# Retention with a routed expert layer: one pool of four PSUM banks for outputs, transposes and states, the router's tasks in other places of a batch, and an order of its own for the first batch

## The chip, the cores and the metric

The kernel runs on one core of a Trainium2 chip. The metric is the time of one execution on the device in microseconds (us), the median over several runs. Below, PE is TensorE (matmuls; PEld its weight loads), DVE is VectorE, ACT is ScalarE, POOL is GpSimd, and SP issues most of the DMA transfers, in its own order.

## The reference

All arrays are float32. A retention layer (attention without softmax, with a decay per head) feeds a layer of eight experts, of which each token uses one.

```python
# q, k, v: (8 batches, 8 heads, 576 positions, 64)
scores = (1 / np.sqrt(64)) * np.matmul(q, k.transpose(0, 1, 3, 2))
gamma = 1.0 - 2.0 ** (-5.0 - np.arange(8))
rel = pos[:, None] - pos[None, :]
Dmat = np.where(rel >= 0, gamma[:, None, None] ** rel, 0.0)
attn = np.matmul(scores * Dmat, v)
x = attn.transpose(0, 2, 1, 3).reshape(4608, 512)        # tokens

xn = x / (norm(x) + 1e-6);  en = expert_emb / (norm(expert_emb) + 1e-6)
logits = xn @ en.T / tau                                 # (4608, 8)
expert_idx = argmax(logits);  gate_w = softmax(logits)[expert_idx]
for e in range(8):                                       # w1: 512 x 1024, w2: 1024 x 512
    out[mask] = gate_w[mask, None] * (np.maximum(x[mask] @ w1[e], 0) @ w2[e])
```

## The kernel before

The work has two stages. In the **batch stage** the eight batches are worked through one after the other. A batch has four head pairs p (two heads side by side on 128 partitions) and four chunks c of 128 positions with a tail of 64. For each pair, `emit_A` (L582) multiplies k and q of each chunk, and DVE multiplies the result with the decay (L591) into a tile `raw`. `emit_O` (L640) multiplies that with v into an output bank. `emit_U` (L609) forms each chunk's state from k and v; ACT copies the first (L619) and DVE sums the others (L621) into `Tst`, so that `Tst[c]` holds all chunks up to c. `emit_S` (L657) adds state times query to the output banks, and ACT copies these to the token tiles `xT` and `xC` (L665 to L668). The tail goes through `emit_At` (L677), a product on DVE that gives `pt` (L679), and `emit_Ot` (L692, L695). POOL scales the queries (`scale_q`, L571) and the keys (`scale_k`, L552) with powers of gamma; for the queries it first builds the table `gsb` (L514). In batch 0 the keys aren't loaded: PE transposes them out of the q/k tiles (`turn_k`, L560), and DVE scales them (L562). `build_E` makes the scaled expert embeddings `E32` (L527 to L537; the reciprocal norm goes through a power on POOL, L533). `keep_warm` issues small matmuls that only keep PE busy.

Between these stand the **router's tasks** for the batch before: `route_logits` (L736), `route_tile` (four transposes L716, a copy to `y` L720, a store of 128 tokens L722, a sum of squares on ACT L724), `route_turn` (L749, reduced on DVE L752), `route_head` (on DVE, L175 to L183, the largest logit), `route_rank` (PE L234 to L238, then DVE L241 to L261), `route_onehot` (L269 to L284) and `route_table` (L297, added on DVE L308). With the last table, rows of x are gathered for the first expert (`gather`, L336).

In the **expert stage** each expert has five tiles of 128 rows; mm1 (L393) and mm2 (L884) multiply in three passes of split float32 weights. ACT and DVE split the weights as they arrive (`wsplit_tasks`, L149 and L150); those of the first expert's w1 are split within the batch stage.

The order on PE is the order in which the program is written (`manual_schedule` for PE). On the other engines the scheduler orders by the program and by when it thinks that inputs are there; each engine then works in a fixed order, and so does SP. A tile of a pool takes the slot that the scheduler gave it and waits for the reader of the tile that was there. PSUM has eight banks: four for `psa` (names a), two for `pso` (outputs, o), two for `psm` (everything else, m).

## Time and profile before

| | |
|---|---|
| median of 3 runs | 656.71 us (655.44 to 658.6) |
| profiled execution | 653.69 us, span of its instructions 651.9 us |
| PE busy | 614.0 us, 94% of the span |
| DVE, ACT, POOL busy | 322.9, 240.4, 211.2 us |
| first decay matmul (L582) of batches 1, 2, 3, 4, 5, 6, 7 | 43.26, 63.26, 87.35, 107.02, 128.56, 147.92, 168.32 us |
| mean granted clock of PE | 0.984 |

The profiled execution's own time lies under the median of the runs by 3.0 us. Times in the trace count from the start of the span. A batch is taken to begin with its first decay matmul.

### The profile page before, as it was taken

Reading aid. Unit: us, or ns where it says so; the run is one execution under the profiler, and the core shown is the slowest. Engines: PE = TensorE matmul, PEld = TensorE weight load, DVE = VectorE, ACT = ScalarE, POOL = GpSimd, SP = SyncE. Lnnn points to the kernel's source line nnn. Section 1 sums busy time; section 2 is a strip of 40 time slices with the busy share of each in tenths; the row PEclk is TensorE's granted clock in tenths of the full one; section 3 lists DMA queues with packets and bytes.
Section 4 is the critical chain, followed back from the end, with each engine's and each line's share of the span. In section 5 each row is a group of like instructions: output and inputs, shape, how many; then the busy total and the mean of one; then the engine's idle time right before and its main releaser. Section 6 shows DMA issues by size and latency. Waiting matters only on the chain. (4 is left out here: it accounts for less than half of the span.)

```text
span 651.9 us, 12713 instructions
## 1 busy us (share of the span) xinstructions
PE 614.0 (94%) x5273; PEld 549.4 (84%) x5273; DVE 322.9 (50%) x612; ACT 240.4 (37%) x457; POOL 211.2 (32%) x190
## 2 busy tenths in 40 slices
PE   4779789999879999999999999999999999999996
PEld 4768677888759898988998998899899889989985
DVE  2455667556546777581465167157336706822200
ACT  0124363444534455442443234143233514422211
POOL 0853335422134663503323240350324135010011
PEclk9879999999989999999999999999999999999999
DMA  8848997757225789565159148526704833610001
GB/s 310 330 166 315 310 336 264 266 206 276 83 81 179 217 208 306 151 164 210 46 115 285 58 120 173 193 71 135 270 31 114 260 111 98 139 57 25 1 33 44
DMA packets 73997, 110.08 MB, mean 169 GB/s; under 512 B 44714, under 2 KB 45774, under 8 KB 72144
## 3 DMA queue, kind: packets, MB, share of 16 engines
q1 hardware_dynamic: 66256, 89.28, 43.9%
q0 software_dynamic: 7680, 19.95, 9.2%
q8 instruction: 42, 0.69, 0.5%
q14 instruction: 19, 0.16, 0.1%
HBM read 80.62 MB, written 19.94 MB: 154 GB/s over the span
## 5 line engine op out<-in xcount | busy, mean ns | idle before, releaser
L393 PE MATMUL a<-xs,wslot 128*128 128x384 f32 (+1 forms) x1536 | 228.2, 310 | 0.2 <-ACT xs L358 0.2
L393 PEld LDWEIGHTS a<-xs,wslot 128*128 128x128 f32 x1536 | 225.8, 189 | 1.2 <-ACT xs L358 0.5
L884 PE MATMUL o<-wslot,hs 128*128 128x512 f32 (+1 forms) x984 | 222.0, 386 | 0.0
L884 PEld LDWEIGHTS o<-wslot,hs 128*128 128x128 f32 x984 | 181.1, 188 | 38.3
L858 DVE SCALAR_TENSOR_TENSOR hs<-a,hs 128x384 fp32r<-128x384 f32 (+1 forms) x128 | 62.6, 490 | 166.9 <-ACT hs L857 166.2
L892 POOL DMA_INDIRECT out<-y,sid x40 | 43.7, 1092 | 223.9 <-ACT y L891 195.0
L857 ACT ACTIVATE hs<-a 128x384 fp32r<-128x384 f32 (+1 forms) x128 | 55.9, 438 | 125.0 <-PE a L393 124.4
L150 DVE TENSOR_TENSOR wslot<-raw,wslot 128x1024 fp32r<-128x1024 f32 x64 | 78.2, 1222 | 31.0 <-ACT wslot L149 31.0
L149 ACT CAST wslot<-raw 128x1024 fp32r<-128x1024 f32 x64 | 66.8, 1043 | 51.4 <-DMA raw<-w 51.4
L891 ACT ACTIVATE y<-o,gt 128x512 f32<-128x512 f32 (+1 forms) x41 | 27.6, 676 | 109.4 <-PE o L884 82.3
L336 POOL DMA_INDIRECT raw<-xd,gid x40 | 41.7, 1043 | 72.8 <-DVE wslot L150 38.4
L571 POOL TENSOR_TENSOR qkt<-qkt,gsb 128x448 f32<-128x448 f32 x32 | 36.5, 1159 | 68.4 <-PE a L582 68.3
L591 DVE TENSOR_TENSOR raw<-a,cs 128x512 f32<-128x512 f32 x64 | 39.9, 681 | 28.8 <-PE a L582 28.8
L347 POOL DMA_INDIRECT gt<-gd,gid x40 | 49.7, 1244 | 12.2 <-issue 11.9
L640 PE MATMUL o<-raw,vt 128*64 128x128 f32 x512 | 35.2, 284 | 8.5 <-DVE raw L591 8.2
L640 PEld LDWEIGHTS o<-raw,vt 128*64 128x64 f32 x512 | 30.0, 142 | 11.4 <-issue 9.3
L552 POOL TENSOR_TENSOR kt<-kt,cs 128x512 f32<-128x512 f32 x28 | 28.3, 1039 | 29.4 <-DMA kt<-kv 29.4
L582 PE MATMUL a<-qkt 64*128 64x128 f32 x512 | 33.2, 279 | 2.2 <-DMA qkt<-qk 2.2
L582 PEld LDWEIGHTS a<-qkt 64*128 64x128 f32 x512 | 29.9, 188 | 4.7 <-DMA qkt<-qk 2.4
L381 DVE COPY raw<-raw 128x1024 uint16<-128x1024 uint16 x37 | 28.1, 781 | 3.6 <-DMA raw<-raw 3.6
L720 ACT COPY y<-m 128x512 f32<-128x512 f32 x34 | 19.4, 585 | 22.3 <-PE m L716 14.4
L374 DVE COPY raw<-raw 128x1024 uint16<-128x1024 uint16 x37 | 26.1, 718 | 3.1 <-DMA raw<-xd,gid 3.1
(128 smaller groups left out, 418.6 us busy)
## 6 DMA issues: line engine op xcount, KB each, us to landing
raw<-w SPq DMA_DIRECT2D x64, 512.0 KB, 5.1
qkt<-qk SPq DMA_DIRECT2D x32, 576.0 KB, 6.4
xd<-y SPq DMA_DIRECT2D x36, 256.0 KB, 4.3
vt<-kv SPq DMA_DIRECT2D x7, 1152.0 KB, 7.1
kt<-kv SPq DMA_DIRECT2D x7, 1024.0 KB, 6.0
vt<-kv SPq DMA_DIRECT2D x4, 256.0 KB, 6.1
cs<-cst SPq DMA_DIRECT2D x5, 128.0 KB, 5.2
raw<-xd,gid POOLq DMA_INDIRECT x40, 3.6
```

What stands on the lines that cost most here:

```text
L149: nc.scalar.copy(hi, raw)
L150: nc.vector.tensor_tensor(out=sl[:, 1, c * 1024 : (c + 1) * 1024], in0=raw, in1=hi.bitcast(F32), op=ALU.subtract)
L336: return nc.gpsimd.indirect_dma_start(out=t[:, :DM], out_offset=None, in_=xd[:rows, :], in_offset=bass.IndirectOffsetOnAxis(ap=gid[:, a : ...
L347: nc.gpsimd.indirect_dma_start(out=g[:, i : i + 1], out_offset=None, in_=gd[:, :], in_offset=bass.IndirectOffsetOnAxis(ap=gid[:, a : a + 1 ...
L393: nc.tensor.matmul(ps[:, :n], w[:, ws, d, f * P : (f + 1) * P], x[:, xsp, d, :], start=(d == 0 and k == 0), stop=(d == NP - 1 and k == 2),)
L582: nc.tensor.matmul(ps[h][:, c * P : (c + 1) * P], t[hs, 1, c * P : (c + 1) * P], t[hs, 0, c * P : (c + 1) * P], start=True, stop=True,)
L591: nc.vector.tensor_tensor(out=pm[:, h], in0=ps[h].rearrange("p (c n) -> p c n", c=NCH), in1=decay[:, 2 * p + h].unsqueeze(1).broadcast_to( ...
L640: nc.tensor.matmul(po[h * D : (h + 1) * D, c * P : (c + 1) * P], v[:, c, 2 * p + h, :], pm[:, h, c, :], start=(c == 0), stop=False,)
L857: a = nc.scalar.activation(hi, ps[:, :n], AF.Relu)
L858: v = nc.vector.scalar_tensor_tensor(out=hs[:, 1, f, o : o + n], in0=ps[:, :n], scalar=0.0, in1=hi.bitcast(F32), op0=ALU.max, op1=ALU.subt ...
L884: nc.tensor.matmul(ps[:, :step], hs[:, hsp, f, i * P : (i + 1) * P], w[:, ws, f, n : n + step], start=(f == 0 and k == 0), stop=(f == NF - ...
L892: nc.gpsimd.indirect_dma_start(out=out[:, :], out_offset=bass.IndirectOffsetOnAxis(ap=sid[:, a : a + 1], axis=0), in_=y, in_offset=None, b ...
```

## The change

The two pools `pso` and `psm` become one pool of four banks. The second state tile `Tst` goes, and `y` has five buffers instead of three. The constants that only the batch stage uses get a tile of their own, `cd`, in the batch stage's memory.

`emit_U(b)` moves from batch b-1 into batch b, ahead of `emit_O(b, 0)`. The keys are loaded at other times through this: their buffer is free when an earlier U has read it. The router's tasks stand in named slots of a batch: logits and two tiles, then ranks, ahead of U; turn, a tile, the head and the table of the batch before that ahead of the outputs of pairs 2 and 3; the other tiles at the end. The squares L724 of a slot stand behind all its copies. For batch 6 the tasks come earlier: logits and two tiles already at its own end. The splits of the first weights move from batches 1 to 4 into batches 4 and 5.

Batch 0 has an order of its own: `build_E` first, then two `turn_k`, the outputs of pairs 0 and 1, then pairs 2 and 3. The expert embeddings and tau are loaded third and fourth from the start, the constants of `gsb` ahead of the fourth q/k tile.

PE at the start of batch 0, behind the first decay matmuls and the warm ones. Names: qkt a q/k tile, kt keys, vt values, raw decay products, sq squares of the embeddings. Before:

```order
L560 MATMUL m<-ident,qkt 128x128 x16
L609 MATMUL m<-vt,kt 64x64 x32
L640 MATMUL o<-raw,vt 64x128 x16
L657 MATMUL o<-qkt,Tst_197 64x128 x12
L530 MATMUL m<-sq,onef 128x8 x4
L582 MATMUL a<-qkt 128x128 x16
```

After:

```order
L530 MATMUL m<-sq,onef 128x8 x4
L560 MATMUL m<-ident,qkt 128x128 x8
L640 MATMUL m<-raw,vt 64x128 x16
L582 MATMUL a<-qkt 128x128 x16
L560 MATMUL m<-ident,qkt 128x128 x8
L609 MATMUL m<-vt,kt 64x64 x32
L657 MATMUL m<-qkt,Tst 64x128 x12
```

The embeddings' matmul, one half of the transposes and the first outputs now stand ahead of the states.

DVE at the same place, before:

```order
L591 TENSOR_TENSOR raw<-a,cs 128x512 x4
L527 TENSOR_TENSOR sq<-emb 128x32
L562 TENSOR_TENSOR kt<-m,cs 128x4x128 x4
L621 TENSOR_TENSOR Tst_197<-m,Tst_197 128x256 x3
L532 COPY en<-m 128x8
L534 TENSOR_SCALAR en<-en,taub 128x8
L535 RECIPROCAL en<-en 128x8
L537 TENSOR_TENSOR E_204<-emb,en 128x8 x4
L591 TENSOR_TENSOR raw<-a,cs 128x512 x4
```

After:

```order
L527 TENSOR_TENSOR sq<-emb 128x32
L591 TENSOR_TENSOR raw<-a,cd 128x512 x4
L532 COPY en<-m 128x8
L534 TENSOR_SCALAR en<-en,taub 128x8
L535 RECIPROCAL en<-en 128x8
L537 TENSOR_TENSOR E_201<-emb,en 128x8 x4
L591 TENSOR_TENSOR raw<-a,cd 128x512 x4
L562 TENSOR_TENSOR kt<-m,cs 128x4x128 x4
L621 TENSOR_TENSOR Tst<-m,Tst 128x256 x3
```

The embedding's chain (sq, en, E) now stands ahead of the second half of the decay products, and the keys kt behind them.

DVE in batch 3 from the sums of the states to the next batch (tab the slot table; L_all, mx, w, wm, oh, s belong to the head). Before:

```order
L621 TENSOR_TENSOR Tst_197<-m,Tst_197 128x256 x3
L679 TENSOR_TENSOR pt<-m,cs 128x256
L308 TENSOR_TENSOR tab<-m,tab 128x80
L752 TENSOR_REDUCE L_all<-m 128x32
L175 TENSOR_REDUCE mx<-L_all 128x4
L176 TENSOR_TENSOR L_all<-L_all,mx 128x32
L178 SCALAR_TENSOR_TENSOR w<-L_all,wme 128x32
L180 TENSOR_REDUCE wm<-w 128x4
L182 TENSOR_TENSOR oh<-wm,wme 128x32
L183 TENSOR_SCALAR tok_all<-wm 128x4
L241 TENSOR_REDUCE s_1466<-oh 128x8
```

After:

```order
L621 TENSOR_TENSOR Tst<-m,Tst 128x256 x3
L591 TENSOR_TENSOR raw<-a,cd 128x512 x4
L759 TENSOR_REDUCE L_all<-m 128x32
L308 TENSOR_TENSOR tab<-m,tab 128x80
L175 TENSOR_REDUCE mx<-L_all 128x4
L176 TENSOR_TENSOR L_all<-L_all,mx 128x32
L178 SCALAR_TENSOR_TENSOR w<-L_all,wme 128x32
L180 TENSOR_REDUCE wm<-w 128x4
L182 TENSOR_TENSOR oh<-wm,wme 128x32
L183 TENSOR_SCALAR tok_all<-wm 128x4
L241 TENSOR_REDUCE s_1425<-oh 128x8
L679 TENSOR_TENSOR pt<-m,cd 128x256
```

The tail product pt stood ahead of the turn's reduction, the table and the head; now it stands behind them.

The diff, cut to its core (line numbers in the text are those of the kernel before; behind the change the tile's copy is still L720, its squares are L730, the turn L756 and L759, the logits L743):

```diff
-    my = ctx.enter_context(tc.tile_pool(name="my", bufs=3))
+    my = ctx.enter_context(tc.tile_pool(name="my", bufs=5))
     psa = ctx.enter_context(tc.tile_pool(name="psa", bufs=4, space=PSUM))
-    pso = ctx.enter_context(tc.tile_pool(name="pso", bufs=2, space=PSUM))
-    psm = ctx.enter_context(tc.tile_pool(name="psm", bufs=2, space=PSUM))
+    psm = ctx.enter_context(tc.tile_pool(name="psm", bufs=4, space=PSUM))
...
         load_qk(0, 0)
         load_decay(0)
-        nc.sync.dma_start(out=cs[:, :_FIRST], in_=cst[:, :_FIRST])
+        nc.sync.dma_start(out=cs, in_=cst[:, :_FIRST])
+        nc.sync.dma_start(out=emb, in_=embT)
+        nc.sync.dma_start(out=taub, in_=tau.rearrange("(o n) -> o n", o=1).broadcast_to([P, 1]))
         load_qk(0, 1)
         load_decay(1)
         load_v(0, True)
         load_qk(0, 2)
         load_decay(2)
+        o = _C["g1"][0]
+        nc.sync.dma_start(out=cd[:, o - _FIRST :], in_=cst[:, o:])
         load_qk(0, 3)
         load_decay(3)
-        o = _C["g1"][0]
-        nc.sync.dma_start(out=cs[:, o:], in_=cst[:, o:])
         load_decay(4)
         kt[0] = a1.tile([P, KW], F32, name="kt", bufs=2)
-        nc.sync.dma_start(out=emb, in_=embT)
-        nc.sync.dma_start(out=taub, in_=tau.rearrange("(o n) -> o n", o=1).broadcast_to([P, 1]))
...
-        Tst = [ap.tile([P, NCH, NP, D], F32, name=f"Tst{i}") for i in range(2)]
+        Tst = ap.tile([P, NCH, NP, D], F32, name="Tst")
...
-                po = Po[b, p] = pso.tile([P, 512], F32, name="o")
+                po = Po[b, p] = psm.tile([P, 512], F32, name="m")
...
-            junk = a2.tile([P, DM], BF16, name="junk", bufs=1)
-            nc.scalar.activation(junk, xw, AF.Square, accum_out=ss_all[:, t : t + 1])
+            squares.append((xw, t))
...
-            first, second = owed or ([], [])
-            owed[:] = [rank], [table]
-            if b == B - 2:
...
-            return [[logits] + first + tiles[:2], second + [turn, head] + tiles[2:]]
+            if b == B - 2:
+                gathers = [lambda i=i: gather(0, i, group_tiles(B - 1)[0] * P) for i in range(3)]
+                return {
+                    (b, 3): [logits] + tiles[:2] + [sq],
+                    (b + 1, 0): [turn] + tiles[2:3] + [head, sq],
+                    (b + 1, 1): [rank, onehot] + tiles[3:] + [sq],
+                    (b + 1, 2): [],
+                    (b + 1, 4): [table, lambda: slots_to_tokens(0, 3)] + gathers + [route_bump],
+                }
+            return {
+                (b + 1, 0): [logits] + tiles[:2] + [sq],
+                (b + 1, 2): [turn] + tiles[2:3] + [head, sq],
+                (b + 1, 3): tiles[3:] + [sq],
+                (b + 2, 0): [rank, onehot],
+                (b + 2, 2): [table],
+            }
...
         for b in range(B):
-            for g in range(2):
-                if b + 1 < B:
-                    load_qk(b + 1, 2 * g)
-                    if g == 0:
-                        load_v(b + 1)
-                        load_k(b + 1)
-                        scale_k(b + 1)
-                    load_qk(b + 1, 2 * g + 1)
-                for p in (2 * g, 2 * g + 1):
+            if b + 1 < B:
+                load_qk(b + 1, 0)
+                load_qk(b + 1, 1)
+                load_v(b + 1)
+                load_k(b + 1)
+            for p in (0, 1):
+                emit_A(b, p)
+                scale_q(b, p)
+            if b == 0:
+                keep_warm(NW2)
+                build_E()
+                turn_k(0)
+                turn_k(1)
+                emit_O(0, 0)
+                for p in (2, 3):
+                    emit_A(0, p)
+                    scale_q(0, p)
+                turn_k(2)
+                turn_k(3)
+                emit_U(0)
+            else:
+                slot(b, 0)
+                emit_U(b)
+                emit_O(b, 0)
+            emit_S(b, 0)
+            if b + 1 < B:
+                load_qk(b + 1, 2)
+                load_qk(b + 1, 3)
+                scale_k(b + 1)
+            slot(b, 1)
+            if b > 0:
+                for p in (2, 3):
                     emit_A(b, p)
                     scale_q(b, p)
-
-                if b == 0 and g == 0:
-                    keep_warm(NW2)
-                    for p in range(NP):
-                        turn_k(p)
-                    emit_U(0)
-                if g == 0:
-                    slot()
-                elif b + 1 < B:
-                    emit_U(b + 1)
-                else:
-                    slot()
-                emit_O(b, g)
-                if g == 1:
-                    emit_At(b)
-                emit_S(b, g)
-                if b == 0 and g == 0:
-                    build_E()
-                if g == 0:
-                    if b == B - 1:
-                        slot()
-                else:
-                    emit_Ot(b)
-                    if b < B - 1:
-                        slot()
-                if b > 0 and wq:
-                    wq.pop(0)()
-            if b < B - 1:
-                tasks += route_tasks(b)
+            slot(b, 2)
+            emit_O(b, 1)
+            slot(b, 4)
+            emit_At(b)
+            emit_S(b, 1)
+            emit_Ot(b)
+            slot(b, 3)
+            if b > 3 and wq:
+                wq.pop(0)()
+                wq.pop(0)()
+        assert not slots
...
-                ps = pso.tile([P, 512], F32, name="o")
+                ps = psm.tile([P, 512], F32, name="m")
```

More of the change, by code (lines that the diff above doesn't have):

```diff
@@ L722, in route_tile, with route_squares @@
             nc.sync.dma_start(out=xd[t * P : (t + 1) * P, :], in_=xw)
-            junk = a2.tile([P, DM], BF16, name="junk", bufs=1)
-            nc.scalar.activation(junk, xw, AF.Square, accum_out=ss_all[:, t : t + 1])
+            squares.append((xw, t))
+        squares = []
+        def route_squares():
+            for xw, t in squares:
+                junk = a2.tile([P, DM], BF16, name="junk", bufs=1)
+                nc.scalar.activation(junk, xw, AF.Square, accum_out=ss_all[:, t : t + 1])
+            squares.clear()
         ltb = {}
@@ L771, in route_tasks @@
             if b == B - 2:
-                return [
-                    [logits] + first + tiles[:2] + [turn, head] + second,
-                    tiles[2:3] + [rank],
-                    tiles[3:] + [table, lambda: slots_to_tokens(0, 3)]
-                    + [lambda i=i: gather(0, i, group_tiles(B - 1)[0] * P) for i in range(3)]
-                    + [route_bump],
-                ]
-            return [[logits] + first + tiles[:2], second + [turn, head] + tiles[2:]]
-        tasks = []
+                gathers = [lambda i=i: gather(0, i, group_tiles(B - 1)[0] * P) for i in range(3)]
@@ L782, in retention_moe, with slot @@
+        slots = {}
+        for b in reversed(range(B - 1)):
+            for k, v in route_slots(b).items():
+                slots.setdefault(k, []).extend(v)
         wq = wsplit_tasks(0)
-        def slot():
-            if tasks:
-                for task in tasks.pop(0):
-                    task()
+        def slot(b, k):
+            for task in slots.pop((b, k), ()):
+                task()
         ordered = tc.manual_schedule(engines={mybir.EngineType.PE})
```

29 lines of the change are left out of this document (16 added, 13 removed).

## The prediction

> **What bounds the kernel now.** I read the span by stage first: busy time of each engine in four stretches, cut where the first decay matmul of batch 1 and of batch 7 starts (43.26 and 168.32) and where the expert matmuls run without a break (203.15). After the stretch and its length stand PE, PEld, DVE, ACT and POOL busy, the granted clock, the DMA share and GB/s.
>
> ```profile
> 0.00:43.26 43.26, 28.46 (x432) 26.10 (x432) 17.32 (x38) 4.37 (x7) 21.84 (x25) 0.84 0.69 258
> 43.26:168.32 125.06, 113.54 (x1987) 97.25 (x1983) 75.12 (x177) 58.02 (x137) 42.95 (x40) 1.00 0.77 273
> 168.32:203.15 34.83, 29.89 (x358) 23.55 (x358) 18.32 (x59) 18.01 (x46) 8.23 (x7) 0.95 0.30 106
> 203.15:651.90 448.75, 442.11 (x2508) 402.47 (x2505) 212.19 (x338) 159.96 (x269) 138.22 (x118) 1.00 0.48 136
> ```
>
> The last stretch is 69% of the span, with PE busy in 442 of 448.75 us at full clock. The change gives its outputs four banks instead of two; there is nothing there to win, and I cost it at nothing. All that can move lies in the first 203 us: PE idles 14.8 us in the first stretch, whose clock is 0.84, 11.5 us in the six batches 1 to 6, 4.9 us in the rest. The list of waits, for PE between 43 and 189 us, names the largest:
>
> ```profile
> PE m L716 <- DVE t L248: 5.6, 5, 1.9
> ```
>
> Token-tile transposes (L716) wait for a bank that holds the ranks until L248 has read them, behind four decay products on DVE. In the first batch the timeline in order of time shows two holes of PE (start, length, work, idle time before it and its releaser):
>
> ```profile
> 15.46 3.61 POOL L514 TENSOR_TENSOR gsb<-cs 128x448 f32<-128x448 f32 x4 [15.04 <-DMA emb<-embT]
> 16.05 0.39 DVE L527 TENSOR_TENSOR sq<-emb 128x32 f32<-128x32 f32 x1 [5.54 <-DMA emb<-embT]
> 16.36 1.28 DVE L562 TENSOR_TENSOR kt<-m,cs 128x512 f32<-128x512 f32 x2
> 17.09 1.97 PE L560 MATMUL m<-ident,qkt 128*128 128x128 f32 x8 [6.22 <-DVE kt L562]
> 18.99 2.93 PE L609 MATMUL m<-vt,kt 128*64 128x64 f32 x64
> 28.10 1.67 POOL L533 TENSOR_TENSOR en<-en,half 128x8 f32<-128x8 f32 x1
> 31.17 3.81 DVE L537 TENSOR_TENSOR E<-emb,en 128x8 f32<-128x8 f32 x4
> 35.73 4.18 PE L640 MATMUL o<-raw,vt 128*64 128x128 f32 x32 [5.61 <-DVE raw L591]
> 43.26 2.06 PE L582 MATMUL a<-qkt 64*128 64x128 f32 x32
> ```
>
> The first hole ends at 17.09: turn_k needs a bank that L562 frees, and L562 stands on DVE behind the squares of the expert embeddings, the seventeenth load on SP. The second ends at 35.73: the output matmuls wait for decay products queued on DVE behind the gate vector's power on POOL (28.10) and four tiny products (31.17) that took 3.81 us while POOL was scaling.
>
> **The change, part by part.** *First batch.* Durations for a walk through its new order:
>
> ```profile
> 8.02 1.16 PE L582 MATMUL a<-qkt 64*128 64x128 f32 x16 [2.22 <-DMA qkt<-qk]
> 9.22 1.29 DVE L591 TENSOR_TENSOR raw<-a,cs 128x512 f32<-128x512 f32 x2 [2.01 <-PE a L582]
> 9.83 1.04 PE L560 MATMUL m<-ident,qkt 128*128 128x128 f32 x8
> 21.75 1.92 PE L640 MATMUL o<-raw,vt 128*64 128x128 f32 x32
> 23.60 1.53 PE L657 MATMUL o<-qkt,Tst 64*64 64x128 f32 x24
> 25.05 1.06 PE L530 MATMUL m<-sq,onef 128*128 128x8 f32 x8
> 28.03 2.08 PE L609 MATMUL m<-vt,kt 128*64 128x64 f32 x64
> ```
>
> The embeddings and tau now precede the second q/k tile on SP, so I put A(0,1) 0.3 late, at 8.3. Twelve warm matmuls follow as before, then build_E (1.06, new here), then two turn_k (1.04): instead of 9.83 the turns start at 11.2, and O(0,0) at 12.2; its 1.92 end at 14.1, A(0,2) and A(0,3) (2.06) at 16.2. The power starts on POOL near 11.4 and ends at 13.1 (1.67); the growth factors gsb, whose constants now load before the fourth q/k tile, follow until 16.7 (3.61). So the tiny products again meet a busy POOL: 1.4 us after the power (as from 29.77 to 31.17) plus 3.81 gives 18.3. Only then come the decay products of pairs 2 and 3 (2 x 1.29: 20.9) and the four key products (2 x 1.28: 23.4). With all four banks held, the last two turn_k wait for the first two key products, so PE is idle from 16.2 to about 21.5, and U(0) ends near 25.5 (2.08 warm, 2.93 cold). The sums let S(0,0) end at 27.4, O(0,1) at 29.3. From the end of O(0,1) to batch 1 took 43.26 - 39.91 = 3.35 before. Batch 1 then starts at 33: **10.3 us earlier**, of which 2.08 is U(1), now done in batch 1. If the tiny products are not held, 30; if cold PE and late loads add up, 37. The fourth q/k tile now loads behind the constants of gsb; PE wants it only at 15. The keys of batch 2 load only after U(0), and hold POOL for the queries of batch 1: 25.5 + 7.3 to land (below) + 4.04 + 2.24 is 39, and S(1,0) wants them at 41.
>
> *Batches 1 to 6* took 125.06 us. How short a batch is without its waits, for an odd and an even one:
>
> ```profile
> 128.56 2.06 PE L582 MATMUL a<-qkt 64*128 64x128 f32 x32
> 132.77 1.09 PE L716 MATMUL m<-ident,xT 128*128 128x128 f32 x8 [0.91 <-DVE t L248]
> 147.92 2.06 PE L582 MATMUL a<-qkt 64*128 64x128 f32 x32
> 151.67 0.18 PE L234 MATMUL m<-oh,stri 128*128 128x32 bf16 x1 [0.48 <-ACT lt L739]
> 165.37 0.77 PE L749 MATMUL m<-ident,lt 128*128 128x128 f32 x5 [0.22 <-ACT xC L700]
> 166.41 1.09 PE L716 MATMUL m<-ident,xT 128*128 128x128 f32 x8 [0.28 <-DVE L_all L752]
> 168.32 2.06 PE L582 MATMUL a<-qkt 64*128 64x128 f32 x32
> ```
>
> Batch 5 took 19.36 with a wait of 0.91, so 18.4; batch 6 took 20.40 with 0.48, 0.22 and 0.28, so 19.4. Three of each make 113.4: **11.6 us** of waits and slower stretches go if nothing replaces them. I think they do go: U(b) now stands between the ranks and O(b,0), so nobody waits for the bank of the ranks, and the weight splits, which put DVE behind a load in batches 1 and 2, move to batches 4 and 5. Each batch still has one U, so that is even. The new wait is on DVE: the head of the router (L175 to L241) stood behind the tail product pt and now stands in front of it, and PE needs pt for the tail outputs L692.
>
> ```profile
> 156.22 2.06 PE L582 MATMUL a<-qkt 64*128 64x128 f32 x32
> 157.41 2.48 DVE L591 TENSOR_TENSOR raw<-a,cs 128x512 f32<-128x512 f32 x4 [3.24 <-PE a L582]
> 162.70 0.42 DVE L679 TENSOR_TENSOR pt<-m,cs 128x256 f32<-128x256 f32 x1 [1.48 <-PE m L677]
> 163.80 0.28 PE L692 MATMUL m<-pt,vt 64*64 64x64 f32 x4
> ```
>
> From the decay matmuls of pairs 2 and 3 (156.22) to L692 were 7.58 us with a U of 2.08 in them; without it, and with turn and one tile added (L716, eight transposes in 1.09, so about 1.1 for both), PE arrives 6.6 us after 156.22. DVE starts its products 1.19 us after PE and needs 2.48 for them: 3.67. Then the head:
>
> ```profile
> 85.09 0.39 DVE L752 TENSOR_REDUCE L_all<-m 128x32 f32<-128x128 f32 x2 [0.64 <-PE m L749]
> 89.03 0.21 DVE L241 TENSOR_REDUCE s<-oh 128x8 f32<-128x40 bf16 x1
> 166.06 0.39 DVE L752 TENSOR_REDUCE L_all<-m 128x32 f32<-128x128 f32 x2 [0.64 <-PE m L749]
> 167.65 0.23 DVE L241 TENSOR_REDUCE s<-oh 128x8 f32<-128x40 bf16 x1
> ```
>
> First and last row of the head: 4.15 us with POOL scaling keys (L552, below), 1.82 without. So pt (0.42) is there at 8.2 or at 5.9: a wait of 1.6 per batch, or none. Which? POOL scales the keys of two batches ahead in these very microseconds:
>
> ```profile
> 77.77 0.33 SPq L446 DMA_DIRECT2D kt<-kv  x1
> 85.04 4.04 POOL L552 TENSOR_TENSOR kt<-kt,cs 128x512 f32<-128x512 f32 x4 [7.85 <-DMA kt<-kv]
> 89.05 2.24 POOL L571 TENSOR_TENSOR qkt<-qkt,gsb 128x448 f32<-128x448 f32 x2
> ```
>
> The keys' load was issued at 77.77, as U had just freed the buffer, and POOL began 7.3 us later. U(b) now ends some 6.5 us into the batch (2.06, an estimated 2.4 for logits, two tiles and ranks, 2.08), so POOL starts near 14; O and S (1.92 + 1.53) bring the next decay matmuls to 10, and the head starts at 10 + 3.67. They meet in batches 1 to 5. The first reductions may still be ahead of POOL, so I take 1.1 instead of 1.6: **+5.5** (0 to 8.2).
>
> The Trainium skill, "SBUF — State Buffer", "Who interferes with whom", says that a DVE instruction with two SBUF inputs, or in a 2-port mode, is blocked for the whole of a GpSimd instruction that reads SBUF, and that reductions and instructions with one SBUF input are not. By that rule L176, L178, L182 and L183 could each lose a whole scaling, and the term would be +16.8 where the rows give at most +8.2, the sum -2 instead of -13.3. The 4.15 above decide against it: each operation there lost only the rest of a scaling.
>
> *Splits.* Four casts stand on ACT ahead of copies out of PSUM in batches 4 and 5:
>
> ```profile
> L149 ACT CAST wslot<-raw 128x1024 fp32r<-128x1024 f32 x64 | 66.8, 1043 | 51.4 <-DMA raw<-w 51.4
> ```
>
> At 1.04 each that is 0 to 4.2; ACT was busy 58 of 125 us, so I take **+1**. *Batch 7 and after:* U(7) comes in (**+2.1**, L609); logits and two tiles go to batch 6, even; its waits for the gathered rows stay, since the slot table still ends behind the last decay products. *Costed at nothing:* squares behind copies (two squares now stand on ACT ahead of U's first copy, which S(b,0) wants only after O(b,0)), five y buffers, the cd tile, one Tst (U(b) writes it after batch b-1 has read it), q/k loads at other places of SP (eight buffers, a batch ahead). If that cover goes, their price is that of the second rival.
>
> Sum: -10.3 - 11.6 + 5.5 + 1 + 2.1 = -13.3. The profiled execution took 653.69 (span 651.9), so 640.4; the median of the runs is 3.0 above it, so **643.4**.
>
> **The rivals.** (a) *No collision:* keys land later than the head. For it: 166.06 shows the head in 1.82. Against: the load follows U at once. 643.4 - 5.5 = 638. (b) *The batches win nothing:* four banks in turn tie every step to the reader four tiles back, and ACT's squares and copies become the waits. For it: the total number of banks is the same. Against: before, two banks served all small tiles. Then 11.6 - 5.5 - 1 is lost: 648.5. (c) *Full holds:* four operations of the head each lose a whole scaling, 4.04 / 4 = 1.01: the head takes 1.82 + 4.04 = 5.86, pt comes at 3.67 + 5.86 + 0.42 = 9.95, PE waits 3.35 in each of five batches, 16.8 instead of 5.5: 654.7. Against: 4.15 with POOL scaling throughout. (The skill's rule above would allow it.) (d) *The first batch does not do what it says:* DVE's chain (tiny products, then decay, then keys) also moves U behind 25.5, and only 4 us are won: 649.5. (e) *Slower:* keys late. POOL is in order, so keys of b+2 that land late hold the queries of b+1 (2.24), which S(b+1,0) needs about 8.4 us into its batch. By the rows keys land 7.3 us after U, and POOL is through with keys and queries (4.04 + 2.24) some 2 us into the next batch at most, so this decides only when landing takes 6 to 7 us longer, 14 instead of 7.3; each further us costs five. To undo 13.3 and add 0.5% takes 3.3 us more: landing after 17 us gives 660.
>
> **How the numbers follow.** Forecast 0.42; (a) 0.20; (b) 0.18; (c) 0.07; (d) 0.07; (e) 0.06. No change within 0.5% (3.3 us, about what the measurement can tell) means 653.4 to 660. The forecast, (a), (b) and (d) are below: 0.87. (c) is no change, 0.07; (e) is slower, 0.06. The range takes in (a) with the first batch at 30 instead of 33 (635), less what splits may save, and (b) and (d) with a little on top: 633 to 652.
>
> **What would show it.** Right: the first L582 of batch 1 near 33; PE holes before 21.5 and before L692 in batches 1 to 5, released by pt, about 1 us each; no wait of L716 for L248; batch 7 starting near 155; the expert stage unchanged at 449. Wrong: batch 1 after 37; L609 or L640 waiting for copies on ACT in every batch; L657 waiting for POOL's queries.

## The result, and the profile after

The changed kernel took 632.86 us in the median of four runs (631.27 to 634.45), beside 656.08 for the kernel before on the same chip: a ratio of 0.9641 with a 95% interval of 0.9602 to 0.9681. The forecast was 643.4 with a range of 633 to 652; the median lies at its lower end, 0.1 us outside. The sign was right; the gain is 23 us instead of 13. The profiled execution took 632.18, its span is 630.4, so 21.5 less than the 651.9 before.

First the stretches, cut where the same work starts: the first decay matmul of batch 1, that of batch 7, and the first mm2. The last two stretches of before (the first two stand in the prediction), with the columns as there:

```profile
168.32:216.40 48.08, 42.98 (x437) 36.18 (x437) 28.89 (x92) 24.01 (x57) 16.36 (x10) 0.96 0.37 128
216.40:651.90 435.50, 429.01 (x2425) 389.83 (x2424) 201.62 (x306) 153.97 (x257) 130.09 (x115) 1.00 0.47 135
```

And the four of after:

```profile
0.00:31.75 31.75, 26.48 (x367) 24.13 (x367) 12.47 (x35) 4.00 (x6) 14.21 (x18) 0.89 0.87 319
31.75:149.63 117.88, 113.42 (x2004) 99.75 (x2000) 68.98 (x177) 58.82 (x141) 53.78 (x48) 0.99 0.83 301
149.63:194.48 44.85, 42.03 (x484) 38.44 (x484) 28.66 (x95) 22.15 (x54) 15.72 (x10) 0.96 0.39 131
194.48:630.40 435.92, 429.21 (x2425) 389.82 (x2424) 201.75 (x306) 153.69 (x257) 132.75 (x115) 1.00 0.47 135
```

The first batch gave 11.5 us, batches 1 to 6 gave 7.2, batch 7 with the passage to the experts 3.2, and the expert stage took 0.4 more. PE is busy for nearly the same time in batches 1 to 6 (113.54 and 113.42), but the span there shrank to 117.88: the idle time is what went. The list of waits after, for PE between 31 and 182 us:

```profile
PE m L716 <- ACT xT L665: 2.2, 1, 2.2
PE m L640 <- DVE L_all L759: 1.8, 3, 0.6
PE m L640 <- DVE raw L591: 1.5, 1, 1.5
```

No wait of L716 for L248 is left, and none of L692 for pt, which the prediction had put in its place. The largest one left is behind a weight split on ACT. The first batch in order of time:

```profile
13.40 1.67 POOL L533 TENSOR_TENSOR en<-en,half 128x8 f32<-128x8 f32 x1 [12.98 <-DVE en L532]
15.60 1.15 DVE L537 TENSOR_TENSOR E<-emb,en 128x8 f32<-128x8 f32 x4
15.67 3.67 POOL L514 TENSOR_TENSOR gsb<-cd 128x448 f32<-128x448 f32 x4 [0.61 <-DMA cd<-cst]
19.51 1.28 DVE L562 TENSOR_TENSOR kt<-m,cs 128x512 f32<-128x512 f32 x2
20.34 1.22 PE L560 MATMUL m<-ident,qkt 128*128 128x128 f32 x8 [2.06 <-DVE kt L562]
31.75 2.06 PE L582 MATMUL a<-qkt 64*128 64x128 f32 x32
```

PE's hole is where it was expected, ahead of the last two turns (L560), but 2.06 long instead of 5.3. The tiny products L537 took 1.15 instead of 3.81. They began at 15.60, and POOL began the growth factors (L514) at 15.67, held until then by the load of their constants: one of the four products took 0.91 us beside the first factor, the other three some 0.16 each.

The head and the tail product in batch 1, with the keys' load ahead of them and POOL's scaling behind:

```profile
38.98 0.48 SPq L445 DMA_DIRECT2D kt<-kv  x1
40.98 2.06 PE L582 MATMUL a<-qkt 64*128 64x128 f32 x32
44.57 0.28 DVE L759 TENSOR_REDUCE L_all<-m 128x32 f32<-128x128 f32 x1
46.01 0.21 DVE L241 TENSOR_REDUCE s<-oh 128x8 f32<-128x32 bf16 x1
46.61 0.42 DVE L679 TENSOR_TENSOR pt<-m,cd 128x256 f32<-128x256 f32 x1 [0.19 <-PE m L677]
47.71 0.28 PE L692 MATMUL m<-pt,vt 64*64 64x64 f32 x4
49.15 4.05 POOL L552 TENSOR_TENSOR kt<-kt,cs 128x512 f32<-128x512 f32 x4 [4.66 <-DMA kt<-kv]
```

The head (L759 to L241) ran in 1.65 us, and pt ended at 47.03, 0.68 before L692. POOL took the keys up at 49.15: issued 7.2 us into the batch and 10.2 on their way. The prediction had 6.5 and 7.3, which put POOL beside the head. In batches 1 to 5 POOL began 8.5 to 10.2 us after the issue, and 1.1 to 2.9 us after the end of the head.

### The profile page after: what moved, and what is told of

It reads as the page before. It is cut to its first block, busy times and chain, and to the rows that moved or that the text cites. A ratio compares the mean times of both kernels' runs of the same rounds, so it can differ in the third digit from the quotient of the medians.

```text
span 630.4 us, 12840 instructions
## 1 busy us (share of the span) xinstructions
PE 611.1 (97%) x5273; PEld 552.1 (88%) x5273; DVE 311.9 (49%) x612; ACT 238.7 (38%) x457; POOL 216.5 (34%) x190
## 5 line engine op out<-in xcount | busy, mean ns | idle before, releaser
L905 PE MATMUL m<-wslot,hs 128*128 128x512 f32 (+1 forms) x984 | 222.0, 386 | 0.0
L905 PEld LDWEIGHTS m<-wslot,hs 128*128 128x128 f32 x984 | 181.1, 188 | 38.3
L150 DVE TENSOR_TENSOR wslot<-raw,wslot 128x1024 fp32r<-128x1024 f32 x64 | 80.8, 1263 | 32.5 <-ACT wslot L149 31.3
L912 ACT ACTIVATE y<-m,gt 128x512 f32<-128x512 f32 (+1 forms) x41 | 27.6, 676 | 108.4 <-PE m L905 89.7
L591 DVE TENSOR_TENSOR raw<-a,cd 128x512 f32<-128x512 f32 x64 | 40.1, 684 | 39.0 <-PE a L582 39.0
L552 POOL TENSOR_TENSOR kt<-kt,cs 128x512 f32<-128x512 f32 x28 | 30.3, 1115 | 21.9 <-DMA kt<-kv 20.6
L582 PE MATMUL a<-qkt 64*128 64x128 f32 x512 | 35.6, 291 | 2.2 <-DMA qkt<-qk 2.1
L582 PEld LDWEIGHTS a<-qkt 64*128 64x128 f32 x512 | 32.1, 199 | 5.4 <-DMA qkt<-qk 2.6
L640 PE MATMUL m<-raw,vt 128*64 128x128 f32 x512 | 31.6, 275 | 3.3 <-DVE L_all L759 1.8
L640 PEld LDWEIGHTS m<-raw,vt 128*64 128x64 f32 x512 | 27.8, 137 | 4.8 <-DVE L_all L759 2.2
L657 PE MATMUL m<-qkt,Tst 64*64 64x128 f32 x384 | 26.1, 283 | 0.1
```

What stands on the lines that cost most here:

```text
L150: nc.vector.tensor_tensor(out=sl[:, 1, c * 1024 : (c + 1) * 1024], in0=raw, in1=hi.bitcast(F32), op=ALU.subtract)
L582: nc.tensor.matmul(ps[h][:, c * P : (c + 1) * P], t[hs, 1, c * P : (c + 1) * P], t[hs, 0, c * P : (c + 1) * P], start=True, stop=True,)
L591: nc.vector.tensor_tensor(out=pm[:, h], in0=ps[h].rearrange("p (c n) -> p c n", c=NCH), in1=decay[:, 2 * p + h].unsqueeze(1).broadcast_to( ...
L640: nc.tensor.matmul(po[h * D : (h + 1) * D, c * P : (c + 1) * P], v[:, c, 2 * p + h, :], pm[:, h, c, :], start=(c == 0), stop=False,)
L905: nc.tensor.matmul(ps[:, :step], hs[:, hsp, f, i * P : (i + 1) * P], w[:, ws, f, n : n + step], start=(f == 0 and k == 0), stop=(f == NF - ...
```

## The experiments

Each run's time is a median beside the kernel before on the same chip (656 to 659 there); the changed kernel is 632.86, and 632.64 in a second set. Executions of one kernel spread by some us, along with PE's granted clock (629.22 us at 0.995 and 634.86 at 0.986 in the second set), so medians less than about 3 us apart are not told apart here. Batches 1 to 3 of the changed kernel, which hold no weight splits, took 54.69 us in both of its profiles and are a steadier measure. Where a kernel has a line more or less, the numbers behind it in its profile are one higher or lower.

**The changed kernel again.**

> The changed kernel as it is, for comparison on the same chip, and a second profile of its first batch. If the tiny embedding products L537 meet the growth factors on POOL in some executions and not in others, then either 1.15 us for the four and batch 1 at 31.75 as in the first profile, or 3.5 us and batch 1 at 34 to 35 as in the run with the busy POOL.

632.64 (629.22 to 634.86), ratio 0.961 (0.957 to 0.965). In this execution the power stood 2 us earlier on POOL (11.26 instead of 13.40), and the products were through before the constants came:

```profile
13.46 0.40 DVE L537 TENSOR_TENSOR E<-emb,en 128x8 f32<-128x8 f32 x4
15.05 3.62 POOL L514 TENSOR_TENSOR gsb<-cd 128x448 f32<-128x448 f32 x4 [2.12 <-DMA cd<-cst]
```

Batch 1 then started at 30.90. So the first batch is a matter of what comes first, load or power, and it varies from run to run; what the power's time hangs on stands in the part on the prediction.

**Four more products on POOL while the head runs** (out is a scratch tile).

```diff
+            if 0 < b < B - 1:
+                for p in range(NP):
+                    nc.gpsimd.tensor_tensor(out=scr, in0=qkt[b, 3][:, 0, P:], in1=gsb[:, p, :], op=ALU.mult)
             slot(b, 2)
```

> The changed kernel with four more products of 128x448 on POOL (into a scratch tile) behind the queries of pair 3 in batches 1 to 6, so that POOL is busy while the router's head runs on DVE: the collision of the prediction made on purpose. The slack from the end of the tail product (47.03) to the tail outputs (47.71) is 0.68 us. By the prediction's rows (head 4.15 us with POOL scaling, 1.82 without) the head is 2.3 longer, the tail outputs wait about 1.6 in six batches: +10, 643. By full holds (each of four operations of the head loses a whole product of 1.12) 3.8 in six batches: +23, 656. If nothing collides: 633. The keys behind the last of these products start up to 1.1 us later than their data, which the queries of the next batch have to spare.

636.47 (633.41 to 641.18): 3.6 more. The profile has two things to show. In the first batch the factors' constants had landed, POOL began right behind the power, and the tiny products met it from the start. In batch 2 the head met the added products:

```profile
14.87 3.61 POOL L515 TENSOR_TENSOR gsb<-cd 128x448 f32<-128x448 f32 x4
16.10 3.49 DVE L538 TENSOR_TENSOR E<-emb,en 128x8 f32<-128x8 f32 x4
66.69 3.56 POOL L842 TENSOR_TENSOR scr<-qkt,gsb 128x448 f32<-128x448 f32 x3
67.35 0.53 DVE L176 TENSOR_TENSOR L_all<-L_all,mx 128x40 f32<-128x40 f32 x1
67.91 1.18 DVE L178 SCALAR_TENSOR_TENSOR w<-L_all,wme 128x40 f32<-128x40 f32 x1
70.48 0.41 DVE L680 TENSOR_TENSOR pt<-m,cd 128x256 f32<-128x256 f32 x1
70.95 0.33 PE L693 MATMUL m<-pt,vt 64*64 64x64 f32 x4
```

The products took 3.49 for four, and batch 1 started at 34.98, 3.2 later than in the first profile, though nothing was changed there. That is the prediction's collision of the tiny products, and the edit didn't ask for it. Over batches 1 to 6 the stretch was 119.33 beside 117.88 and 115.94, so 1.5 to 3.4 more. The head's operations that read SBUF twice lost parts of a product (0.53 and 1.18 instead of 0.20), the reductions lost nothing, and L693 waited 0.27 us. It did so in three batches. In batch 1 it waited 0.80: there the cast L243 stands between the head and pt on DVE and took 0.91 instead of 0.17, so that pt ended at 51.76, 0.15 before L693. (The list of waits puts these 0.80 down to a copy on ACT that ended at 51.81.) In two batches it didn't wait. So the wait that was put at 1.1 to 1.6 per batch is 0.8 at most when it is made on purpose, and 1.6 in all.

**Two pools of two banks again, PE's order kept.**

```diff
-    psm = ctx.enter_context(tc.tile_pool(name="psm", bufs=4, space=PSUM))
+    pso = ctx.enter_context(tc.tile_pool(name="pso", bufs=2, space=PSUM))
+    psm = ctx.enter_context(tc.tile_pool(name="psm", bufs=2, space=PSUM))
```

> The changed kernel with two pools of two banks again (outputs; everything else), all orders kept. Theory A: the places of tasks and states took the waits away, the pool did not; then 633 to 636. Theory B: the common pool of four is what lets the small tiles follow each other; with two banks, a tile waits for the copy or the reduction of the tile two places ahead, five or six times a batch at 0.3 to 0.5 us, some 2 us in each of six batches: 643 to 648, with waits of the tile transposes and of the states for copies on ACT.

648.43 (645.91 to 650.85), ratio 0.989 (0.9826 to 0.9953): 15.6 lost, theory B and a little more. Batch 1 started at 31.56, so nothing is lost in the first batch; batches 1 to 6 took 130 us, 12 more than with four banks and 5 more than the kernel before. Some of the waits that came, from the list for PE:

```profile
PE m L693 <- DVE pt L680: 4.5, 2, 3.0
PE m L717 <- DVE L_all L760: 3.5, 3, 1.2
PE m L717 <- ACT lt L747: 1.8, 5, 0.5
PE m L610 <- DVE t L249: 1.5, 5, 0.3
```

The longest of them, and the stretch of batches 1 to 6:

```profile
135.45 0.33 PE L693 MATMUL m<-pt,vt 64*64 64x64 f32 x4 [3.04 <-DVE pt L680]
```

```profile
31.56:161.53 129.97, 115.36 (x2003) 98.31 (x1999) 68.31 (x177) 61.16 (x144) 52.99 (x48) 1.00 0.75 275
```

The tiles wait for the reader of the tile two places back, 0.3 to 1.2 us at a time; in batches 1 to 3 that comes to 4.6 us (59.29 beside 54.69). The largest item is another. L693 waited 1.5 and 3.0 us in batches 4 and 5 for pt, which on DVE stands here behind the subtraction of a weight split (L151), and that waited 2.0 and 3.5 us for its cast. With four banks pt stood ahead of it. So the edit changed the scheduler's order on DVE too, and of the 15.6 us these 4.5 are not the turn of the banks: some 11 are left for it (an estimate from these two waits).

**The kernel before with one pool of four banks, nothing else.**

> The kernel before with nothing changed but the pool: outputs, transposes and states take turns in four banks instead of two and two. Theory A (the banks alone): the changed kernel lost 15.5 us when it was given two pools again, so here 12 to 15 are won: 642 to 645, with no wait of the tile transposes for the ranks' reader L248. Theory B (banks and places together): in the old order the ranks' bank is asked for again only four tiles later, but the outputs stand in the same turn and wait for copies on ACT; half is won: 648 to 651. Theory C (the banks matter only in the new order): 655 to 660.

651.1 (648.57 to 656.57), ratio 0.9919 (0.9878 to 0.9959): 5.2 won, theory B. In its profile batches 1 to 6 are only 1.2 us shorter than in the kernel before (123.87 and 125.06), and batch 7 with the passage to the experts 2.2. The two largest of PE's waits over the whole span (in batches 1 to 6 the second is 2.2 in two):

```profile
PE m L639 <- DVE t L247: 6.7, 4, 2.0
PE m L639 <- DVE raw L590: 6.4, 4, 3.8
```

And the timeline of DVE and PE around the start of batch 2 (65.59):

```profile
64.83 0.29 DVE L751 TENSOR_REDUCE L_all<-m 128x32 f32<-128x128 f32 x1 [2.00 <-PE m L748]
69.39 2.48 DVE L590 TENSOR_TENSOR raw<-a,cs 128x512 f32<-128x512 f32 x4
71.78 0.18 DVE L247 TENSOR_TENSOR t<-m,oh 128x32 f32<-128x32 f32 x1
72.01 2.91 PE L639 MATMUL m<-raw,vt 128*64 128x128 f32 x32 [2.00 <-DVE t L247]
```

The outputs of pair 1 now stand four tiles behind the ranks and wait for L247 (L248 of before), which waits on DVE behind decay products (L590), and these behind the head, which runs while POOL scales.

So the banks are worth 5 us in the old order and 11 to 15.6 in the new one. Which piece of the new order matters was asked of four kernels.

**The same with the ranks behind the two tiles** (`[logits] + tiles[:2] + first`).

> The kernel before with the one pool of four banks, and the ranks behind the two token tiles instead of ahead of them (nothing else of the new order). With four banks in the old places the output matmuls of pair 1 take over the bank of the ranks and waited 6.7 us for its reader L248 in four batches. Theory (the place of the ranks): these waits go, 644 to 646. Rival (the head): L248 was late because the head and the four decay products behind it are late; the outputs then wait for the decay products themselves, and 2 to 3 us at most are won: 648 to 651.

657.74 (653.1 to 661.39), ratio 0.999 (0.9951 to 1.0028): all but 0.8 of the 5.2 is lost again, a smaller gain than either expectation. The two largest of PE's waits over the whole span (in batches 1 to 6 the first is 8.0 in three), and one copy of a token tile on ACT:

```profile
PE m L639 <- DVE raw L590: 12.3, 5, 5.5
PE m L639 <- ACT y L719: 7.3, 2, 4.3
```

```profile
101.06 0.59 ACT L719 COPY y<-m 128x512 f32<-128x512 f32 x1 [3.92 <-DMA xd<-y]
```

The wait for L247 is gone, but waits for decay products (behind the head, and once 5.46 us behind a weight split on DVE) and for the copies of token tiles took its place. The copy had waited 3.92 us for the store of an earlier y, of which this kernel has three buffers. Several pieces of the old order hold it, one behind the other.

**The changed kernel with the ranks ahead of the tiles.**

```diff
-                (b + 1, 0): [logits] + tiles[:2] + [sq],
+                (b + 1, 0): [logits],
+                (b + 1, 5): tiles[:2] + [sq],
```

> The changed kernel with the ranks ahead of the two token tiles again, right behind the logits; all else kept. The second half of the states then takes over the ranks' bank. Theory (the place of the ranks): it waits for L248, 0.5 to 1 us in each of five batches: 635 to 638. Rival (the head): in the new order no head stands ahead of the decay products, L248 comes some 3.9 us into the batch and the states' second half is reached 5.3 us into it: no wait, 631 to 634.

634.3 (632.76 to 638.75), batches 1 to 6 in 117.54 and batches 1 to 3 in 54.74: nothing. The states waited for L248 once, 1.70 us in batch 6, and in no other batch. The rival holds; the place of the ranks is worth next to nothing in the new order.

**The changed kernel with turn and head at the end of the batch.**

```diff
-                (b + 1, 2): [turn] + tiles[2:3] + [head, sq],
-                (b + 1, 3): tiles[3:] + [sq],
+                (b + 1, 2): tiles[2:3] + [sq],
+                (b + 1, 3): [turn, head] + tiles[3:] + [sq],
```

> The changed kernel with turn and head at the end of the batch again, behind the tail outputs: the tail product then stands ahead of the head on DVE, and the head ahead of the next batch's decay products, while POOL scales keys. Theory (the head's place made the gain): the head takes 3 to 4 us there, the decay products start that much later, and the outputs of pair 0 wait 1 to 2 us in each of five batches: 638 to 643. Rival (logits, tiles, ranks and states ahead of the outputs leave DVE the time): 632 to 635.

636.01 (633.99 to 638.19): 3.2 more, between the two. Batches 1 to 6 took 120.9, and batches 1 to 3 took 56.61, 1.9 more than after. Across the start of batch 2 (48.89) the head now met POOL's scaling in full:

```profile
48.56 0.29 DVE L759 TENSOR_REDUCE L_all<-m 128x32 f32<-128x128 f32 x1 [2.40 <-PE m L756]
49.11 0.90 DVE L176 TENSOR_TENSOR L_all<-L_all,mx 128x32 f32<-128x32 f32 x1
51.93 1.05 DVE L183 TENSOR_SCALAR tok_all<-wm 128x4 f32<-128x4 f32 x1
53.13 0.95 DVE L243 CAST run<-s 128x8 bf16<-128x8 f32 x1
54.00 2.47 DVE L591 TENSOR_TENSOR raw<-a,cd 128x512 f32<-128x512 f32 x4
48.92 4.04 POOL L552 TENSOR_TENSOR kt<-kt,cs 128x512 f32<-128x512 f32 x4 [5.13 <-DMA kt<-kv]
```

From L759 to the decay products it is 5.44 us; the head itself (L759 to the end of L241) took 4.54 instead of 1.65. By the stretch of batches 1 to 6 in the two profiles of the changed kernel (117.88 and 115.94) this part of the new order is worth 3 to 5 us.

**The changed kernel with the states a batch ahead** (`emit_U(b + 1)` ahead of `emit_O(b, 1)`, two state tiles, three y buffers).

> The changed kernel with the states of the next batch computed a batch ahead, in front of the outputs of pairs 2 and 3 (two state tiles, three y buffers), everything else kept. Theory A (the place of the states is what hides the ranks, and it is what brings the keys' load so late that the head meets no scaling): outputs then stand right behind the ranks, keys land earlier, and the head meets the scaling on POOL, 1 to 2 us in each of five batches: 638 to 643. Theory B (the four banks alone hide both): no change, 632 to 635.

635.48 (633.05 to 637.31), at the upper edge of theory B. Batches 1 to 6 took 117.97, the same as after, but not in the same way: batches 1 to 3 took 56.64, 1.9 more, and in batches 4 and 5 L692 waited 0.9 and 2.1 us for pt, with a weight split ahead of it on DVE. The head met no scaling. So the place of the states with its y buffers is worth some 2 us where no splits stand, and nothing in the sum. Batch 1 started at 36.71, 2.08 of it the states of batch 1 and most of the rest the collision of the tiny products (3.50).

**The first batch in its old order, with the old loads.**

> The changed kernel with the first batch in its old order (four turns of the keys, states, outputs, embeddings behind them) and with the old order of the first loads; the states of batch 1 still stand in batch 1. Theory: the first batch's gain stands by itself. Batch 1 then starts at 43.26 - 2.08 = 41.2 us instead of 31.75, so 9.4 us are lost and the time is about 642.3. Rival: the rest of the gain leans on the early start (loads of batch 1 and 2 fall otherwise); then batches 1 to 6 change too, by 2 us or more, and the time is outside 640 to 645.

645.25 (640.16 to 648.33): 12.4 lost. Batch 1 started at 44.64, 3.4 later than expected; batches 1 to 6 took 118.64, so the gain does stand by itself. Of the 3.4, 2.1 are the states of batch 1: in the kernel before, they ran on PE inside the wait for the decay products, so leaving them out saved nothing. Without them that wait was 7.9 us instead of 5.6. The rest goes with this execution, the longest of the four: between 16 and 30 us its granted clock was 0.70 (0.83 in the kernel before), and the states of batch 0 took 4.83 us instead of 2.93.

**Squares right behind each copy.**

> The changed kernel with the squares of a token tile right behind its copy on ACT again, instead of behind all copies of the slot. Each square takes 0.8 us on ACT, and the next tile's copy then frees its bank 0.8 later. If the banks of the transposes are asked for at once, some 0.5 us in each of 12 places: 636 to 639. If the four banks hide it, as the prediction had it: 631 to 634.

635.08 (634.38 to 636.32). Batches 1 to 6 took 117.20, no more than after; batch 1 started at 35.03, with the tiny products at 3.50. The squares cost nothing there; in the profiled execution all that was lost lies in the first batch.

**The constants of the growth factors behind the fourth q/k tile.**

```diff
-        o = _C["g1"][0]
-        nc.sync.dma_start(out=cd[:, o - _FIRST :], in_=cst[:, o:])
         load_qk(0, 3)
         load_decay(3)
+        o = _C["g1"][0]
+        nc.sync.dma_start(out=cd[:, o - _FIRST :], in_=cst[:, o:])
```

> The changed kernel with the constants of the growth factors loaded behind the fourth q/k tile instead of ahead of it. Theory: the factors then start on POOL 1 to 2 us later, behind the tiny embedding products on DVE, which take 1.15 us in every execution instead of 1.15 or 3.5; batch 1 starts at 31 to 32 and the median falls by 0 to 2 us, with less spread: 631 to 633. Rival: the queries, later by as much, hold the states' outputs of batch 0: +1 to +2, 634 to 635.

631.23 (629.17 to 636.11). In this kernel and the three below that have the edit, the four products took 0.40 us each time. In the ten profiles of the new first batch with the constants ahead they took 0.40 four times, 1.15 once and 3.5 five times. The median alone doesn't tell the 1.4 us from noise.

**The weight splits in other batches** (`if b > 4 and wq` and `if b > 0 and wq`).

> The changed kernel with the four splits of the first weights in batches 5 and 6 instead of 4 and 5. Theory: in batch 4 (DMA share 0.94) two casts on ACT wait for weights and hold the copies out of PSUM, PE stops 2.2 us and the next decay matmuls run at a lower clock (3.42 instead of 2.06), some 4 us in all; batch 6 has a DMA share of 0.59, so the weights are there in time: 628 to 631. Rival: the wait goes along to batch 5 or 6, where the casts stand ahead of the same copies: 632 to 635.

> The changed kernel with the four splits at the ends of batches 1 and 2 instead of 4 and 5. In batches 4 and 5 they cost 4.0 us in the first profile. If any place in the batches costs the same: 632 to 634. If the loads of the first batches leave the weights less room (the old kernel's batch 2 took 24.09 us, 3 to 4 more than its like): the casts wait longer and hold copies and decay products, 635 to 639.

629.89 (629.07 to 633.0) and 634.31 (632.35 to 636.12). Late, batches 4 and 5 took 20.1 and 17.9 instead of 21.9 and 19.3 (21.6 and 17.9 in the second profile of the changed kernel), but batch 6 took 24.7 instead of 22.0: the wait went along. Early, batch 2 took 25.3 instead of 19.2. Four splits cost 6.0 us there and 2.3 to 4.0 in batches 4 and 5 (the two profiles of the changed kernel); no place among the loads was free.

**Three together, and the splits one by one, and last.** All three have the late growth constants and the slot table in `(b + 2, 1)` instead of `(b + 2, 2)`; splits in batches 5 and 6, one in each of 3 to 6, and in 6 and 7.

> The changed kernel with the splits in batches 5 and 6, the growth constants behind the fourth q/k tile, and the slot table's matmuls ahead of the decay matmuls of pairs 2 and 3 instead of behind the turn (then the output matmuls of pair 2 should not wait for the turn's reduction, 0.6 us in each of three batches). If the three add up: 4 + 1 + 1.8 less, 626 to 629. If the table so early waits for its inputs on DVE, the 1.8 come back there: 628 to 631.

> The changed kernel with the growth constants behind the fourth q/k tile, the slot table ahead of the decay matmuls of pairs 2 and 3, and the splits of the first weights one by one at the ends of batches 3 to 6. In the run with two splits in batches 5 and 6, batches 2 to 5 took 18.0 to 18.9 us and batch 6 took 25.3, of which 2.5 were a wait for casts and slow matmuls behind it. Theory: one load instead of two is there before the cast wants it, no copy waits, and batches 4 to 6 lose under 1 us each: 626 to 629. Rival: the load's landing, not the number, sets the wait, now in four batches instead of two: 631 to 634.

> As the run before, but the four splits at the ends of batches 6 and 7. Theory: batch 6 keeps its wait (2 to 4 us) and batch 7 has no loads beside the weights, so one of two waits goes: 627 to 630. Rival: the splits of batch 7 stand on DVE and ACT just where the first expert's matmuls want their weights, and PE waits there: 633 or more.

631.43 (627.91 to 632.61), 630.3 (629.01 to 631.53) and 628.97 (628.39 to 629.25). The early table took the waits of L640 for L759 away (1.8 us after), and batches 2 to 5 of the first took 18.85, 18.00, 18.69 and 17.99; batch 6 with its splits took 25.26. With the splits in batches 6 and 7 that stretch has no idle time left:

```profile
33.41:145.69 112.28, 112.27 (x2003) 98.21 (x1999) 66.33 (x175) 57.45 (x139) 50.01 (x48) 1.00 0.83 306
```

This version has a ratio of 0.9568 (0.9528 to 0.9609) to the kernel before. Its interval overlaps a little with that of the changed kernel; but each of its four runs lies below 629.3, and of ten runs of the changed kernel one does.

## Why the prediction was wrong, step by step

*First batch, -10.3: right in its order, near the number in part by luck.* Batch 1 started at 31.75, forecast 33, bounds 30 to 37. The order was walked through as it came. But the 33 hold the term for the tiny products (1.4 + 3.81), and in the profile they took 1.15. Of the ten profiles with this first batch, the five in which they took 3.5 have batch 1 at 34.31 to 36.46 (leaving out the states of batch 1 where they stand ahead of it), forecast 33; the four with 0.40 have it at 30.90 to 31.56, forecast 30. Which it is hangs on whether the growth factors' constants are there when the power ends, and the power's time went with PE's clock. In the four with 0.40 the mean granted clock of the first 16 us was 1.00 and the twelve warm matmuls took 0.88 us; in the other six it was 0.75 to 0.89 and they took 1.46 or 1.47. The power then began at 13.2 to 15.7 instead of 11.3 to 12.4, and where POOL waited for the constants, they were there at 15.0 to 15.7. A lower clock went with a later batch 1 without the collision too: of the four kernels with late constants, three had 1.00 and batch 1 at 30.40 to 30.65, the one with the splits last had 0.81 and 33.41. No row of before could show which it would be.

*Waits that go, -11.6: too small by 2.4.* With no splits, a batch took 17.58 to 17.88 and 19.23 (the first three), so six take 111 us, 14.0 less. (In the kernel before, the four splits stood in batches 1 and 2, not in 1 to 4; the 14.0 hold what they cost there, and no run separates it.) The step read a batch without its waits as its length less the waits listed (18.4 and 19.4). PE's busy time was longer too. Batch 3 of before has 328 matmuls:

```profile
87.35:107.02 19.67, 18.25 (x328) 15.85 (x328) 11.75 (x30) 9.22 (x25) 7.49 (x8) 1.00 0.81 281
```

and batch 3 of after has the same:

```profile
68.56:86.44 17.88, 17.88 (x328) 15.94 (x328) 10.46 (x30) 9.59 (x26) 6.46 (x7) 1.00 0.88 332
```

0.37 us of busy time went with 1.4 us of idle time, though the matmuls took the same mean time each (278 ns for L582, 274 for L640, 279 for L716, before and after). The records of matmuls in a row overlap (64 of 278 ns in 4.1 us), and a wait breaks that overlap; this would account for the 0.37, but no run isolates it.

*The new wait at L692, +5.5: this is the step that failed.* It was 0. PE's arrival (6.6 into the half, measured 6.73 in batch 1) and DVE's without a collision (5.9, measured 6.05) were right. Wrong was the meeting of the head with POOL's scaling of the keys, which were both put near 14 us into the batch. In batches 1 to 5 the keys' load was issued after 7.2 to 8.4 us instead of 6.5, and POOL began 8.5 to 10.2 us later instead of 7.3, so the head had ended 1.1 to 2.9 us before. The later issue and a head that in batches 1 to 4 came 0.5 to 0.9 us earlier do most of it: with a landing of 7.3, POOL would have begun within 0.3 us of the head's end in each of the five batches. The 7.3 was one row, and the longest of four: the keys of the kernel before took 5.2 to 7.3. Why they now take longer is argued and not isolated: the load is issued right behind two q/k tiles on SP, where in the kernel before, and in the one with the states a batch ahead, 3.4 to 5.6 us lay between, and there POOL began 5.2 to 7.3 us after the issue. The DMA share while the load was on its way doesn't tell the two apart: 0.86 in batch 1 of after, 0.89 in the row of before. Rival (a), at 0.20, was what happened, though its 638 was still 5 too high. And where the collision was made on purpose, L692 waited 0.8 at most instead of 1.6, so the bound of 8.2 was too high as well.

*Splits, +1: too small by 3.* Batch 4 took 2.67 more than batch 2, and batch 5 1.38 more than batch 3, whose tasks are the same (2.32 and 0.00 in the second profile, so there too small by 1.3):

```profile
104.68 1.05 ACT L149 CAST wslot<-raw 128x1024 fp32r<-128x1024 f32 x1 [4.13 <-DMA raw<-w]
106.91 1.07 ACT L665 COPY xT<-m 128x512 f32<-128x512 f32 x2
107.54 0.87 PE L716 MATMUL m<-ident,xT 128*128 128x128 f32 x4 [2.21 <-ACT xT L665]
108.34 3.42 PE L582 MATMUL a<-qkt 64*128 64x128 f32 x32
```

The casts waited for their weights 4.13 us, the copy of the outputs stood behind them, L716 waited for that copy, and the next decay matmuls took 3.42 instead of 2.06 (granted clock 0.85 over the 9.7 us from 108.34). The step had priced the cast (1.04), not what it waits for. The row that the prediction shows said so: 51.4 of ACT's idle time was put down to these loads, 12.1 of it before the four casts in batches 1 and 2.

*Batch 7, +2.1: -0.4.* Batch 6 took 2.8 more with its own tasks, batch 7 and the passage 3.2 less. The states of batch 7 came in as said; idle time of PE there fell from 5.1 to 2.8, where the waits had been taken to stay.

*Costed at nothing:* squares were right by the runs, y buffers and the place of the states to within 2 us (only tried together); the expert stage too (+0.4). The q/k loads at other places of SP were not tried alone; by the step on L692 they may be what moved the landing of the keys.

Measured: -11.5 - 14.0 + 0 + 4.0 - 0.4 + 0.4 = -21.5. (By its own terms rival (d) comes to 649.7, not 649.5.) Rival (b) was wrong the other way round: four banks in turn are what makes the new order pay. What stays open is how the 15.6 us of the banks divide among the waits that return without them, beyond the 4.5 behind the weight splits; and how much of the old order's waits with four banks is due to the head, to the splits and to three y buffers, since only the head was moved alone.

The prediction weighed a rule of the Trainium skill against the 4.15 us of the head beside POOL, and held that each operation loses only the rest of a scaling. With the head at the end of the batch, L176, L178, L182, L183 and the cast L243 lost 0.55 to 0.9 us each, and the three reductions nothing: 4.54 from L759 to the end of L241, nearer to the 4.15 than to the 5.86 of rival (c), but with the losses spread as the rule has it. The Trainium skill, "SBUF — State Buffer", "Who interferes with whom", also counts casts and `tensor_scalar` operations among those that can contend, through their 2-port modes. These traces agree that both can lose time (L183 1.05 and L243 0.95), though they don't show the mode. What kept the rule from counting was the place of the head, clear of POOL's scaling.

## What to carry to other kernels

Banks and order are one resource: in a pool taken in turn each tile waits for the reader of the one that many places back, so a larger common pool and the order of the tasks must be costed together (5.2 us in the old order, 11 to 15.6 in the new one). Don't place a collision by the landing time of one load: read it from every row that has it, ask what stands ahead of it in its queue now, and give both outcomes a price. An edit to a pool can change the scheduler's order on other engines; look at that order before the difference is put down to the pool. A cast that shares an in-order engine with copies out of PSUM costs the lateness of its load, not its own time.

## What of the hardware was not expected

- Operations of DVE on 8 elements per partition took 0.10 us alone (four in 0.40) and 0.87 beside products on POOL (four in 3.49). Which of the two came went with PE's granted clock in the first 16 us: 1.00 in the four executions with 0.40, 0.75 to 0.89 in the five with 3.5, where the power came later and the constants had landed before the products.
- A scalar operation with one tensor input (L183) took 1.05 us and a cast 0.95 beside POOL's scaling, where 0.16 and 0.17 are usual, while products of a PSUM tile with an SBUF one (L591) kept their 0.62 each.
- The same wait was not followed by the same clock. In the first profile a wait of 2.21 us on PE at the end of batch 4 came before decay matmuls of 3.42 instead of 2.06, and the mean granted clock of batch 5 was 0.92 (0.99 or 1.00 in the other five). With the added products on POOL the wait at that place was 2.26 us, in the second profile 1.79, and both times the decay matmuls behind it kept their 2.06. What decides it stays open.
